# A gate's second half moved beside the next unit's first half, and weight pieces prepared one unit ahead

## The chip, the core and the metric

The kernel runs on one core of a Trainium2 chip. Its metric is device time in microseconds, from a run of the whole program. In what follows, PE is the matrix engine, with its weight loads as a lane of their own (PEld), DVE the vector engine, ACT the scalar engine, POOL the GpSimd engine and SP the engine that issues the DMAs.

## What is computed

Three layers follow one another, all in float32. The kernel reaches float32 accuracy by splitting operands into a high part (rounded to the matrix engine's format) and a low part (what the rounding left), and by three matmuls for each product: high by high, high by low, low by high.

```python
# attention without softmax, 4 batches, 8 heads, 576 positions, head size 64
scores = scale * q @ k.T;  ret = scores * decay_mask;  x = (ret @ v)     # 2304 tokens x 512
# first layer, 512 -> 2048 -> 512
h = x @ w_in;  g = h * cos(h);  x = g @ w_out
# second layer, 512 -> 1536 -> 512
xn = x / rms(x) * rms_g
out = (silu(xn @ w_gate) * (xn @ w_val)) @ w_out
```

## The kernel before, in words

The program has three stages: attention with the first units of the first layer beside it (to about 165 us of the span), the rest of the first layer (to about 510 us), and the second layer (to the end). The change is in the first layer.

**Units.** Tokens are cut into tiles of 512 (the last has 256), the 2048 inner columns into 16 blocks of 128. One unit is one block for one tile. There are 80 units, numbered i, in six segments: 0 to 5, 6 to 21, 22 to 31, 32 to 47, 48 to 63 (the tile of 256 tokens) and 64 to 79. For a unit PE makes 12 matmuls for h (lines 211 to 213, "hidden", called H here, tiles h or acc read from xhi and xlo), and three units later 12 matmuls of the product with w_out (same lines, called O here, read from ghi and glo). In steady state PE's order is H of unit i, O of unit i-3, H of unit i+1, O of unit i-2, and so on. H writes one of four rotating PSUM banks.

**Gate.** Between H and O stands the gate g = h cos h, six instructions that hand over from engine to engine (function gate_cos): ACT rounds h / 2 pi to an integer (line 452, called k here), DVE takes the remainder (line 453, r), ACT the sine (line 455), DVE multiplies by h (line 459), ACT casts to the high part (line 461, tile ghi), and DVE takes the low part (line 135, tile glo; on POOL in units 31 and 47).

**Weight pieces.** Beside units 22 to 67 the weights of the second layer, which come as 64-bit words of two floats' parts, are made into float32: 36 pieces, one for each unit except units 31 and 47, every other unit from 48 to 62, and units 64 to 67. A piece is loaded by SP (line 475, 512 KB), ACT takes the size (line 143) and the low word (line 152), DVE does two bit operations (lines 147 and 148), a combination (line 153) and an addition (line 154), and SP stores it to DRAM (line 491). The function piece_steps is a generator; the gate asks for its next part at five points (step()).

**Other work in the same places.** Units 24 to 62 also carry the root-mean-square normalisation of tiles that are done (tile nt, lines 352 to 396), one or two instructions a unit. Units 68 to 79 carry the splitting of second-layer weights and operands into high and low parts, pulled one by one from a list at the same five points: ACT high part (line 541), DVE low part, four POOL additions on z (line 547), ACT high parts of the sums (line 553), DVE low parts, and ACT and DVE splits of x (line 619 and line 135). At units 46, 47, 62 and 63 the next segment's x is split (ACT line 192, DVE line 135).

**What sets the order.** From unit 22 on, ACT, DVE and POOL run exactly in the order in which the program is written; each engine's queue is in order, so an instruction that waits holds up all behind it. The orders of PE and SP are made by a scheduler when the program is built, and are in order too when it runs.

**Buffers.** The gate's working tile r has two buffers, ghi and glo three each; a piece's raw words have three buffers, its working tile t two. Two pieces are loaded ahead.

Of the kernel before, what the change touches and what calls it, by code (L numbers as in the profile page):

```python
# [30 lines left out]
P = 128  # L31
# [54 lines left out]
def body(ctx: ExitStack, tc, qkv, qkr, vr, w1, w2, rg, gq, gk, mask, out):  # L86
# [35 lines left out]
        taken[0] += 1  # L122
        return hidden_tile() if taken[0] % 2 else acc_tile(KC + taken[0] // 2 % 2)

    mask_sb = const.tile([P, P], F32, name="mask_sb")
# [8 lines left out]
    def minus(eng, dst, hi, src):  # L134
        eng.tensor_tensor(dst, src, hi.bitcast(F32), op=ALU.subtract)  # L135
# [6 lines left out]
    def value1(t, words):  # L142
        nc.scalar.activation(t.bitcast(F32), words[..., 1].bitcast(F32), AF.Abs)

    def value2(t):
        size = t.bitcast(F32)
        nc.vector.tensor_scalar(size, size, LEAST, LARGEST, op0=ALU.max, op1=ALU.min)
        nc.vector.tensor_scalar(t, t, 3, 0x3FFFFFF8, op0=ALU.logical_shift_left, op1=ALU.bitwise_and)

    def value3(t, words):  # L150
        low, high = words[..., 0], words[..., 1]
        nc.scalar.activation(low, low.bitcast(U32), AF.Copy, scale=2.0 ** -29)
        nc.vector.scalar_tensor_tensor(t, high, -2 ** 30, t, op0=ALU.bitwise_and, op1=ALU.bitwise_or)  # L153
        nc.vector.tensor_tensor(t, t, low, op=ALU.add)  # L154
# [73 lines left out]
    N = len(chunks)  # L228
    width = lambda c: P if c < NFULL else REST
    ld, sc, total = {}, {}, {}  # L230
    gam0 = ap1.tile([P, NPAIR, P], F32, name="gam0")
    gam = [gam0]
    PRO = NCH
# [30 lines left out]
    def scores(n):  # L264
        b, c = chunks[n]
        w = width(c)
        kt, qt, vv, _ = ld[n]
        v3 = vv[:w].rearrange("p (h d) -> p h d", h=H)
        nc.gpsimd.tensor_tensor(v3, v3, vg_sb[:w, c, :].unsqueeze(2).to_broadcast([w, H, D]), op=ALU.mult)
        ps = [ps_tile().rearrange("p (h i) -> p h i", h=NPAIR) for _ in range(2)]  # L270
        for p in range(NPAIR):
            for hh in range(2):
                r = slice(hh * D, (hh + 1) * D)
                nc.tensor.matmul(ps[hh][:w, p, :w], kt[r, p, :], qt[r, p, :], start=True, stop=True)  # L274
        for hh in range(2):
# [160 lines left out]
        proj(part1("in", f), t, ps)  # L436
        return ps[:, :n]

    def gate_cos(t, f, ps, between=None, eng=nc.gpsimd, beside=None, copies=()):

        def step():
            next(beside)
            if copies:
                copies.pop(0)()

        n = TILES[t][1]
        r = ch.tile([P, 512], F32, tag="t", name="r")
        k = r.bitcast(I32)
        hi = ch.tile([P, 512], F32R, tag="hi", bufs=LAG, name="ghi")
        lo = ch.tile([P, 512], F32R, tag="lo", bufs=LAG, name="glo")  # L450
        k, r, hi, lo = k[:, :n], r[:, :n], hi[:, :n], lo[:, :n]
# [21 lines left out]
    def piece_load(k):  # L473
        loaded[k] = late["cv"].tile([P, DM, 2], I32, tag="raw", name="raw")
        nc.sync.dma_start(loaded[k].rearrange("p c w -> p (c w)"),
                          w2[k // 2, :, k % 2 * DM:(k % 2 + 1) * DM].bitcast(I32))

    def piece_steps(k):
# [215 lines left out]
    for i in range(LAST + LAG):  # L694
        if i == ATT_STEPS:
            att.close()
            late["psh"] = pool("psh", 1, space=PSUM)
            late["wb"] = mid.enter_context(tc.tile_pool(name="wb", bufs=NSLOT_B, reuse_waits="tile"))
        if ATT_STEPS <= i < MANUAL:
            while len(blocks1) < NW1:  # L700
                blocks1.append(Block(w1[len(blocks1)], wa if len(blocks1) < NSLOT_A else late["wb"]))
        more = [n for n in range(chunk, chunk + CHUNKS[i])] if i < ATT_STEPS else []
        for n in more:
            if n + AHEAD < N:
                fetch_chunks(n + AHEAD)
        early_out = LAG <= i < LAST and i - LAG in ENDS
        if i < LAST:
            s, t, f = STEPS[i]
            ps = hidden(t, f)
            if i in ENDS and i + 1 < LAST:  # L710
                if SEGMENTS[s + 1][1]:
                    fetch_x(SEGMENTS[s + 1][0])
                else:
                    split_x(SEGMENTS[s + 1][0], range(KC // 2, KC) if TILES[t][1] < 512 else range(KC))
            elif i + 1 in ENDS and TILES[t][1] < 512:
                split_x(SEGMENTS[s + 1][0], range(KC // 2))
            if early_out:
                out_t(i - LAG)
            gate_cos(t, f, ps, (lambda: scores(more[0] + 1)) if more and more[0] + 1 < N else None,
                     nc.vector if i < MANUAL or i >= 3 * NF1 or begun(i) is not None else nc.gpsimd,  # L720
                     piece_steps(begun(i)) if begun(i) is not None
                     else other_steps(5 if i < LAST - 1 else 2) if i >= LAST - NF1 else iter(range(5)), late.pop("moves", []))
        elif i >= LAST:
            if i == LAST:

                nc.scalar.activation(spare, half_pi, AF.Silu)
            for _ in range(7):
                pull()
        if i >= LAG and not early_out:
            out_t(i - LAG)  # L730
        if more:
            values(more[0])
            if len(more) > 1:
                if more[0] + 2 < N:
                    scores(more[0] + 2)
                values(more[1])
            chunk += len(more)
        if i < MANUAL:

            while converted[0] < min(len(blocks1), CONVERTED[i]):  # L740
                blocks1[converted[0]].convert(temps())
                converted[0] += 1
        if i == 1:
            keep_x(0)
        if i < LAST - NF1 and (i // NF1 != 3 or 0 not in normal):
            idle()
            idle(1, "D" if i % 2 else "A")
        if i >= LAST - NF1 + LAG:
            ahead(i, i - (LAST - NF1 + LAG))
        if i == MANUAL - 1:  # L750
# [5 lines left out]
            piece_load(0)  # L756
            piece_load(1)
            order = ExitStack()
            order.enter_context(tc.manual_schedule(engines=ENGINES))
# [320 lines left out]
```

## Time and profile before

| | us |
|---|---|
| median of 3 runs | 918.08 (917.05 to 923.83) |
| profiled execution, device time | 917.62 |
| its span, first to last instruction | 915.8 |
| time outside the span | 1.8 |
| PE busy | 890.1 (97%) |
| DVE busy | 666.9 (73%) |
| ACT busy | 476.6 (52%) |
| POOL busy | 91.8 (10%) |

The table's busy times are averages over stages with different limits. A matmul's reported length overlaps the next one's, so the distance between two starts tells more of PE than the length does. A wait is given to the event that came last before the instruction began.

### The profile page before, as it was taken

To read this page: it belongs to the slowest core of one execution; us is meant where nothing else is said; L and a number is where in the kernel's file an instruction comes from. 1 tells how busy PE (TensorE), PEld (TensorE's weight loads), DVE (VectorE), ACT (ScalarE), POOL (GpSimd) and SP (SyncE) were. 2 spreads that over 40 slices of the span, in tenths; PEclk is the share of its full clock that TensorE was granted. 3 is DMA by queue.
4 is the path that set the end of the run, shared out by engine and by line. 5 is a ranking of instruction groups with operands and counts; after the bars stand their busy time and mean duration, and the time that the engine had idled before them with its cause. 6 is when DMAs were issued, how large, how long until landed. Compare 5 with 4: busy or idle time off the path is not lost.

```text
span 915.8 us, 14516 instructions
## 1 busy us (share of the span) xinstructions
PE 890.1 (97%) x5610; PEld 802.0 (88%) x5610; DVE 666.9 (73%) x1003; ACT 476.6 (52%) x819; POOL 91.8 (10%) x99
## 2 busy tenths in 40 slices
PE   7799999999999999989998999999999999999998
PEld 6677787887888887988886999999999999999998
DVE  2999887855878887777777689879675589343484
ACT  3666554745665556646656765536433445333341
POOL 2210010000000000000244444300000000000000
PEclk8999999999999999999999999999999999999999
DMA  8972550504434443332477887998877688866693
GB/s 323 395 298 92 191 212 11 198 11 150 138 108 135 138 138 126 117 104 81 162 236 253 290 315 298 334 340 277 266 259 256 221 278 288 278 246 242 220 295 118
DMA packets 61333, 193.20 MB, mean 211 GB/s; under 512 B 5584, under 2 KB 23632, under 8 KB 52688
## 3 DMA queue, kind: packets, MB, share of 16 engines
q1 hardware_dynamic: 61264, 192.27, 61.3%
q8 instruction: 44, 0.72, 0.3%
q14 instruction: 25, 0.20, 0.1%
HBM read 142.97 MB, written 49.28 MB: 210 GB/s over the span
## 4 chain that ended last, share of the span: by engine, by line
PE 67%; DVE 17%; ACT 7%; issue 4%; DMA 3%; POOL 1%; SPq 1%; ACTq 0%; DVEq 0%; POOLq 0%
PE h L833 13%; PE acc L878 13%; PE acc L833 12%; PE acc L211 5%; PE acc L212 4%; PE acc L213 4%; DVE r L459 2%; PE g L274 2%; PE h L878 2%; DVE w L135 2%; DVE r L453 2%; DVE t L153 2%; ACT ghi L461 2%; PE g L304 2%; DVE t L154 2%
## 5 line engine op out<-in xcount | busy, mean ns | idle before, releaser
L833 PE MATMUL acc<-w 128*128 128x384 f32 x720 | 140.1, 335 | 0.5
L833 PE MATMUL h<-w 128*128 128x384 f32 x720 | 139.8, 335 | 0.8 <-DVE SV L815 0.7
L833 PEld LDWEIGHTS h<-w 128*128 128x128 f32 x720 | 126.1, 188 | 2.4 <-DVE SV L815 1.8
L833 PEld LDWEIGHTS acc<-w 128*128 128x128 f32 x720 | 125.6, 188 | 2.4 <-DVE v L821 2.4
L211 PE MATMUL acc<-ghi,w 128*128 128x512 f32 (+1 forms) x320 | 117.7, 374 | 6.5 <-ACT ghi L461 6.5
L212 PE MATMUL acc<-glo,w 128*128 128x512 f32 (+1 forms) x320 | 119.3, 373 | 0.5 <-DVE glo L135 0.4
L213 PE MATMUL acc<-ghi,w 128*128 128x512 f32 (+1 forms) x320 | 119.0, 372 | 0.0
L878 PE MATMUL acc<-w 128*128 128x256 f32 x846 | 104.2, 283 | 0.0
L878 PEld LDWEIGHTS acc<-w 128*128 128x128 f32 x846 | 103.1, 191 | 0.3 <-DVE w L135 0.2
L455 ACT ACTIVATE r<-r,half_pi 128x512 f32<-128x512 f32 (+1 forms) x80 | 54.5, 682 | 65.1 <-DVE r L453 65.0
L547 POOL TENSOR_TENSOR z<-z 128x256 f32<-128x256 f32 x72 | 63.9, 890 | 164.8 <-DVE r L453 85.4
L135 DVE TENSOR_TENSOR glo<-r,ghi 128x512 fp32r<-128x512 f32 (+1 forms) x78 | 51.5, 661 | 39.1 <-ACT ghi L461 38.6
L211 PEld LDWEIGHTS acc<-ghi,w 128*128 128x128 f32 x320 | 59.9, 188 | 18.5 <-ACT ghi L461 7.9
L461 ACT CAST ghi<-r 128x512 fp32r<-128x512 f32 (+1 forms) x80 | 46.2, 578 | 50.2 <-DVE r L459 47.2
L212 PEld LDWEIGHTS acc<-glo,w 128*128 128x128 f32 x320 | 60.8, 190 | 11.4 <-DVE glo L135 1.5
L213 PEld LDWEIGHTS acc<-ghi,w 128*128 128x128 f32 x320 | 60.9, 190 | 10.2
L821 DVE TENSOR_TENSOR v<-s,acc 128x384 f32<-128x384 f32 x54 | 29.8, 552 | 52.8 <-PE acc L833 39.4
L861 ACT CAST w<-SV 128x768 fp32r<-128x768 f32 x55 | 42.4, 832 | 34.1 <-DVE SV L866 18.2
L135 DVE TENSOR_TENSOR w<-SV,w 128x768 fp32r<-128x768 f32 x55 | 50.3, 957 | 13.5 <-ACT w L861 13.5
L799 ACT COPY s<-h 128x384 f32<-128x384 f32 x54 | 25.9, 480 | 56.6 <-PE h L833 55.2
L799 ACT COPY s<-acc 128x384 f32<-128x384 f32 x54 | 26.0, 481 | 49.6 <-PE acc L833 49.5
L815 DVE TENSOR_TENSOR SV<-s,h 128x384 f32<-128x384 f32 x54 | 29.8, 551 | 27.7 <-PE h L833 22.2
(128 smaller groups left out, 1684.7 us busy)
## 6 DMA issues: line engine op xcount, KB each, us to landing
w<-so SPq DMA_DIRECT2D x42, 768.0 KB, 6.2
w<-s SPq DMA_DIRECT2D x24, 1024.0 KB, 4.9
raw<-w_dram SPq DMA_DIRECT2D x36, 512.0 KB, 4.0
w<-s SPq DMA_DIRECT2D x24, 768.0 KB, 4.3
raw<-w_dram SPq DMA_DIRECT2D x16, 1024.0 KB, 6.6
x<-qkv_dram SPq DMA_DIRECT2D x15, 1024.0 KB, 8.8
s<-w SPq DMA_DIRECT2D x12, 1024.0 KB, 6.3
w<-t SPq DMA_DIRECT2D x36, 256.0 KB, 2.3
```

The source lines that it names most:

```text
L135: eng.tensor_tensor(dst, src, hi.bitcast(F32), op=ALU.subtract)
L211: nc.tensor.matmul(dst, a[0], b[0], start=start, stop=False)
L212: nc.tensor.matmul(dst, a[0], b[1], start=False, stop=False)
L213: nc.tensor.matmul(dst, a[1], b[0], start=False, stop=stop)
L455: nc.scalar.activation(r, r, AF.Sin, bias=half_pi, scale=1.0)
L461: nc.scalar.copy(hi, r)
L547: nc.gpsimd.tensor_tensor(z[:, dst], z[:, a], z[:, b], op=op)
L799: nc.scalar.copy(t[:, :HALF], bank)
L815: nc.vector.tensor_tensor(dst, s, bank, op=ALU.add)
L833: nc.tensor.matmul(bank, w[:, wp, kc * P:(kc + 1) * P], x[:, kc], start=k in (0, 1, 3) and kc == 0 and m == 0, stop=kc == 1 and m == 2, sk ...
L861: nc.scalar.copy(t[:, 0], src)
L878: nc.tensor.matmul(bank, s[:, a, i % 2, m * P:(m + 1) * P], wi[:, b], start=start and i == 0 and p == 0 and m % 2 == 0, stop=i == NPR - 1 ...
```

## The change

In units 22 to 79 the gate's last three instructions (product, cast, low part) no longer follow the sine of the same unit. They are kept as `pending` and are written between the first three of the next unit. The low part is always on DVE. After unit 79 a call without a unit finishes what is pending. For units below 22 the order within a unit stays (`apart` is false).

For a weight piece, the two ACT instructions of piece k+1 are written beside the DVE instructions of piece k; three pieces are loaded ahead and t has three buffers. `mask_sb` moves to a pool that is closed after attention. The number of weight steps that unit 79 and the step behind it pull goes from 2 to 5 and from 7 to 9.

```diff
-    def gate_cos(t, f, ps, between=None, eng=nc.gpsimd, beside=None, copies=()):
+    pending = []
+
+    def gate(t, f, ps, beside, copies, between=None, apart=False):
...
-        nc.scalar.activation(k, ps, AF.Identity, bias=quarter, scale=INV_2PI)
-        nc.vector.scalar_tensor_tensor(r, k, -TWO_PI, ps, op0=ALU.mult, op1=ALU.add)
-        step()
-        nc.scalar.activation(r, r, AF.Sin, bias=half_pi, scale=1.0)
-        step()
-        if between:
-            between()
-        nc.vector.tensor_tensor(r, ps, r, op=ALU.mult)
-        step()
-        nc.scalar.copy(hi, r)
-        step()
-        minus(eng, lo, hi, r)
-        step()
-        g_parts[t, f] = hi, lo
...
+        def finish():
+            mult, cast, low = pending.pop()
+            mult()
+            step()
+            return cast, low
...
+            nc.scalar.activation(k, ps, AF.Identity, bias=quarter, scale=INV_2PI)
+            old = finish() if pending else None
+            nc.vector.scalar_tensor_tensor(r, k, -TWO_PI, ps, op0=ALU.mult, op1=ALU.add)
+            step()
+            if old:
+                old[0]()
+                step()
+            nc.scalar.activation(r, r, AF.Sin, bias=half_pi, scale=1.0)
+            step()
+            if old:
+                old[1]()
+                step()
+            pending.append((lambda: nc.vector.tensor_tensor(r, ps, r, op=ALU.mult), cast, low))
...
+        if pending and (ps is None or not apart):
+            cast, low = finish()
+            cast()
+            step()
+            low()
+            step()
...
     def piece_steps(k):
-        j, n = divmod(k, 2)
-        t = late["cv"].tile([P, DM], I32, tag="t", bufs=2, name="t")
-        value1(t, loaded[k])
+        ahead = piece_first(k + 1) if k + 1 < npiece else []
+        t, words = sizes.pop(k), loaded.pop(k)
         yield
         value2(t)
+        for step in ahead[:1]:
+            step()
         yield
         yield
+        for step in ahead[1:]:
+            step()
+        nc.vector.scalar_tensor_tensor(t, words[..., 1], -2 ** 30, t, op0=ALU.bitwise_and, op1=ALU.bitwise_or)
         yield
-        value3(t, loaded.pop(k))
+        nc.vector.tensor_tensor(t, t, words[..., 0], op=ALU.add)
...
-        if k + 2 < npiece:
-            piece_load(k + 2)
+        if k + 3 < npiece:
+            piece_load(k + 3)
```

Three places of the built programs show what moved. The first is DVE in unit 44, a unit of 512 tokens with a piece beside it (r is the gate's tile, t and raw the piece's). Before:

```order
L453 SCALAR_TENSOR_TENSOR r<-r,acc 128x512
L147 TENSOR_SCALAR t<-t 128x512
L148 TENSOR_SCALAR t<-t 128x512
L459 TENSOR_TENSOR r<-acc,r 128x512
L135 TENSOR_TENSOR glo<-r,ghi 128x512
L153 SCALAR_TENSOR_TENSOR t<-raw,t 128x512
L154 ISA t<-raw,t 128x1024
```

and in the changed program:

```order
L481 TENSOR_TENSOR r<-h,r 128x512
L471 SCALAR_TENSOR_TENSOR r<-r,acc 128x512
L146 TENSOR_SCALAR t<-t 128x512
L147 TENSOR_SCALAR t<-t 128x512
L530 SCALAR_TENSOR_TENSOR t<-raw,t 128x512
L134 TENSOR_TENSOR glo<-r,ghi 128x512
L532 ISA t<-raw,t 128x1024
```

The product (now line 481) and the low part (now line 134) are those of unit 43, whose bank is h; the four piece instructions and the remainder stand between them, and the low part stands between the piece's combination (line 530) and its addition (line 532).

The second is ACT in units 78 (bank h) and 79 (bank acc), the last two. Before:

```order
L452 ACTIVATE r<-h,quarter 128x512
L455 ACTIVATE r<-r,half_pi 128x512
L541 CAST w<-z 128x768
L461 CAST ghi<-r 128x512
L619 CAST w<-xall 128x768
L452 ACTIVATE r<-acc,quarter 128x512
L455 ACTIVATE r<-r,half_pi 128x512
L553 CAST w<-z 128x512 x2
L461 CAST ghi<-r 128x512
L726 ACT_TABLE_LOAD
```

and in the changed program:

```order
L469 ACTIVATE r<-h,quarter 128x512
L462 CAST ghi<-r 128x512
L585 CAST w<-z 128x768
L476 ACTIVATE r<-r,half_pi 128x512
L663 CAST w<-xall 128x768
L469 ACTIVATE r<-acc,quarter 128x512
L597 CAST w<-z 128x512 x2
L462 CAST ghi<-r 128x512
L476 ACTIVATE r<-r,half_pi 128x512
L585 CAST w<-z 128x768
L462 CAST ghi<-r 128x512
L770 ACT_TABLE_LOAD
```

The cast of unit 78 moved behind the rounding of unit 79 and behind the two casts of sums (line 597, before line 553), which stood behind it.

The third is PE at the end of the first layer, from the last O of unit 78 on (h<-w 128x384 is the second layer). Before:

```order
L213 MATMUL acc<-ghi,w 128x512
L833 MATMUL h<-w 128x384 x9
L211 MATMUL acc<-ghi,w 128x512 x4
L212 MATMUL acc<-glo,w 128x512
L213 MATMUL acc<-ghi,w 128x512
```

and in the changed program, from the last matmuls of unit 79's O on:

```order
L210 MATMUL acc<-ghi,w 128x512
L211 MATMUL acc<-glo,w 128x512
L212 MATMUL acc<-ghi,w 128x512
L879 MATMUL h<-w 128x384 x30
L879 MATMUL acc<-w 128x384 x12
```

The nine matmuls of the second layer that stood between the O of units 78 and 79 moved behind unit 79's.

## Rows read from the trace of the kernel before

**Rows 1.** The page's first part: busy time, share of the span, instructions of each engine.
```profile
PE 890.1 (97%) x5610; PEld 802.0 (88%) x5610; DVE 666.9 (73%) x1003; ACT 476.6 (52%) x819; POOL 91.8 (10%) x99
```
**Rows 2.** Busy time by stretch: stretch, its length, five engines' busy us, PE clock, DMA share, GB/s.
```profile
340.00:360.00 20.00, 18.14 (x89) 14.97 (x88) 15.49 (x28) 13.39 (x25) 1.30 (x1) 1.00 0.48 147
...
390.00:420.00 30.00, 26.94 (x179) 24.36 (x178) 23.30 (x48) 14.10 (x30) 0.00 (x0) 0.94 0.32 104
...
480.00:510.00 30.00, 26.00 (x108) 20.80 (x106) 21.17 (x29) 20.77 (x34) 12.70 (x16) 0.94 0.79 264
510.00:600.00 90.00, 88.90 (x506) 86.36 (x505) 74.15 (x109) 54.21 (x106) 35.54 (x42) 1.00 0.86 313
```
**Rows 3.** PE in order of time: start, us, instruction, idle before it.
```profile
352.18 0.39 PE L213 MATMUL acc<-ghi,w 128*128 128x512 f32 x1
353.71 0.38 PE L211 MATMUL acc<-xhi,w 128*128 128x256 f32 x1 [1.14 <-ACT xhi L192]
354.82 0.38 PE L212 MATMUL acc<-xhi,w 128*128 128x256 f32 x1 [0.72 <-DVE xhi L135]
```
**Rows 4.** PE in order of time, round 407 and 413 us.
```profile
406.74 0.28 PE L212 MATMUL acc<-glo,w 128*128 128x256 f32 x1
406.86 0.28 PE L213 MATMUL acc<-ghi,w 128*128 128x256 f32 x1
409.48 0.74 PE L211 MATMUL acc<-ghi,w 128*128 128x256 f32 x4 [2.34 <-ACT ghi L461]
...
412.46 0.63 PE L213 MATMUL h<-xhi,w 128*128 128x512 f32 x1
412.88 0.63 PE L211 MATMUL h<-xhi,w 128*128 128x512 f32 x1
```
**Rows 5.** PE in order of time, at the first layer's end.
```profile
497.91 0.39 PE L213 MATMUL acc<-ghi,w 128*128 128x512 f32 x1
501.90 1.20 PE L211 MATMUL acc<-ghi,w 128*128 128x512 f32 x4 [3.61 <-ACT ghi L461]
```
**Rows 6.** DVE in order of time, from one low part to the next (units 42 and 43).
```profile
330.82 0.69 DVE L135 TENSOR_TENSOR glo<-r,ghi 128x512 fp32r<-128x512 f32 x1 [0.74 <-ACT ghi L461]
...
336.43 0.69 DVE L135 TENSOR_TENSOR glo<-r,ghi 128x512 fp32r<-128x512 f32 x1 [0.74 <-ACT ghi L461]
```
**Rows 7.** Busy time by stretch, as in rows 2, of units 38 to 43 and 55 to 61.
```profile
301.30:336.90 35.60, 35.60 (x159) 29.48 (x158) 30.05 (x52) 18.28 (x32) 0.00 (x0) 1.00 0.43 133
384.00:409.00 25.00, 22.42 (x179) 21.41 (x177) 18.90 (x40) 11.61 (x25) 0.00 (x0) 1.00 0.33 113
```
**Rows 8.** DVE from 384 to 409 us by line: busy us, mean ns, idle before, releaser.
```profile
L135 DVE TENSOR_TENSOR glo<-r,ghi 128x256 fp32r<-128x256 f32 x6 | 2.6, 425 | 3.2 <-ACT ghi L461 3.2
...
L459 DVE TENSOR_TENSOR r<-acc,r 128x256 f32<-128x256 f32 x4 | 1.7, 424 | 2.3 <-ACT r L455 2.3
```
**Rows 9.** ACT from 454 to 502.4 us (units 71 to 78) by line.
```profile
L553 ACT CAST w<-z 128x512 fp32r<-128x512 f32 x10 | 5.9, 619 | 10.7 <-POOL z L547 7.6 <-DMA so<-w 3.1
L455 ACT ACTIVATE r<-r,half_pi 128x512 f32<-128x512 f32 x8 | 5.8, 724 | 4.9 <-DVE r L453 4.9
...
L461 ACT CAST ghi<-r 128x512 fp32r<-128x512 f32 x8 | 5.0, 620 | 3.6 <-DVE r L459 3.5
```
**Rows 10.** ACT in order of time, units 77 and 78.
```profile
493.04 0.82 ACT L541 CAST pw<-z 128x768 fp32r<-128x768 f32 x1
...
496.89 1.14 ACT L553 CAST w<-z 128x512 fp32r<-128x512 f32 x2 [2.33 <-POOL z L547]
497.94 0.68 ACT L452 ACTIVATE r<-h,quarter 128x512 int32<-128x512 f32 x1
...
501.23 0.62 ACT L461 CAST ghi<-r 128x512 fp32r<-128x512 f32 x1 [0.41 <-DVE r L459]
```
**Rows 11.** Line 213 on PE: count, ns min/median/max, first and last start.
```profile
L213 PE MATMUL h<-xhi,w x132: 279/389/628, 167.2 to 486.1; 128*128 128x512 f32 x100, 128*128 128x256 f32 x32
```
**Rows 12.** The page's DMA issues: count, KB each, median us from issue to landing.
```profile
raw<-w_dram SPq DMA_DIRECT2D x36, 512.0 KB, 4.0
```

More of the change, by code (lines that the diff above doesn't have):

```diff
@@ L230, in body @@
     ld, sc, total = {}, {}, {}
+    mask_sb = ap1.tile([P, P], F32, name="mask_sb")
     gam0 = ap1.tile([P, NPAIR, P], F32, name="gam0")
@@ L454, in gate_cos, with cast, low @@
-        step()
-        nc.scalar.activation(r, r, AF.Sin, bias=half_pi, scale=1.0)
-        step()
-        if between:
-            between()
-        nc.vector.tensor_tensor(r, ps, r, op=ALU.mult)
-        step()
-        nc.scalar.copy(hi, r)
-        step()
-        minus(eng, lo, hi, r)
-        step()
-        g_parts[t, f] = hi, lo
+        def finish():
[3 more added lines that the diff above has]
+            return cast, low
+        if ps is not None:
+            n = TILES[t][1]
+            r = ch.tile([P, 512], F32, tag="t", name="r")
+            k, r = r.bitcast(I32)[:, :n], r[:, :n]
+            parts = {}
+            def cast():
+                parts["hi"] = ch.tile([P, 512], F32R, tag="hi", bufs=LAG, name="ghi")[:, :n]
+                nc.scalar.copy(parts["hi"], r)
+            def low():
+                parts["lo"] = ch.tile([P, 512], F32R, tag="lo", bufs=LAG, name="glo")[:, :n]
+                minus(nc.vector, parts["lo"], parts["hi"], r)
+                g_parts[t, f] = parts["hi"], parts["lo"]
+            nc.scalar.activation(k, ps, AF.Identity, bias=quarter, scale=INV_2PI)
[11 more added lines that the diff above has]
+            pending.append((lambda: nc.vector.tensor_tensor(r, ps, r, op=ALU.mult), cast, low))
+            if between:
+                between()
@@ L469, in body @@
+        if pending and (ps is None or not apart):
[4 more added lines that the diff above has]
+            step()
+        for _ in beside:
+            pass
+        while copies:
+            copies.pop(0)()
     store = [dram.tile([P, 4, 2 * P], F32, tag=f"w2_{j}", name=f"w2_{j}") for j in range(NW2)]
@@ L476, in piece_load, with piece_first, size, low @@
                           w2[k // 2, :, k % 2 * DM:(k % 2 + 1) * DM].bitcast(I32))
+    sizes = {}
+    def piece_first(k):
+        def size():
+            sizes[k] = late["cv"].tile([P, DM], I32, tag="t", bufs=3, name="t")
+            value1(sizes[k], loaded[k])
+        def low():
+            words = loaded[k]
+            nc.scalar.activation(words[..., 0], words[..., 0].bitcast(U32), AF.Copy, scale=2.0 ** -29)
+        return [size, low]
     def piece_steps(k):
-        j, n = divmod(k, 2)
-        t = late["cv"].tile([P, DM], I32, tag="t", bufs=2, name="t")
-        value1(t, loaded[k])
+        ahead = piece_first(k + 1) if k + 1 < npiece else []
+        t, words = sizes.pop(k), loaded.pop(k)
         yield
         value2(t)
+        for step in ahead[:1]:
+            step()
         yield
         yield
+        for step in ahead[1:]:
+            step()
+        nc.vector.scalar_tensor_tensor(t, words[..., 1], -2 ** 30, t, op0=ALU.bitwise_and, op1=ALU.bitwise_or)
         yield
-        value3(t, loaded.pop(k))
+        nc.vector.tensor_tensor(t, t, words[..., 0], op=ALU.add)
+        j, n = divmod(k, 2)
         where = store[j][:, 2 * n:2 * n + 2] if j % 3 < 2 else store[j][:, 1:3] if n else store[j][:, 0:4:3]
         nc.sync.dma_start(where, t.bitcast(F32).rearrange("p (n c) -> p n c", n=2))
-        if k + 2 < npiece:
-            piece_load(k + 2)
+        if k + 3 < npiece:
+            piece_load(k + 3)
         yield
@@ L718, in body @@
                 out_t(i - LAG)
[L719 to L722, printed above, removed]
+            gate(t, f, ps, piece_steps(begun(i)) if begun(i) is not None
+                 else other_steps(5) if i >= LAST - NF1 else iter(range(5)), late.pop("moves", []),
+                 (lambda: scores(more[0] + 1)) if more and more[0] + 1 < N else None, i >= MANUAL)
         elif i >= LAST:
             if i == LAST:
+                gate(None, None, None, other_steps(2), [])
                 nc.scalar.activation(spare, half_pi, AF.Silu)
@@ L755, in body @@
             late["cv"] = right("cv", 3)
-            piece_load(0)
-            piece_load(1)
+            for k in range(3):
+                piece_load(k)
             order = ExitStack()
+            for step in piece_first(0):
+                step()
             order.enter_context(tc.manual_schedule(engines=ENGINES))
```

7 lines of the change are left out of this document (removed).

## The prediction

> **What bounds the kernel now.** I read the page's busy shares, then the busy times by stretch, then PE, DVE and ACT in order of time where PE stood still. PE is busy 97% of the span [rows 1], so the whole first layer can only win what PE loses there. It loses it at three places [rows 2]. Where two starts of a matmul lie further apart than usual I count the excess; the usual distance is 0.12 us for 256 columns [rows 4], and for 512 it is 35.6 us over 159 matmuls, 0.22 [rows 7].
>
> First, at 352 us PE waits for the split of x: 353.71 - 352.18 - 0.22 and 354.82 - 353.71 - 0.12, together 2.3 us [rows 3]. Second, from 400 to 414 us it waits for gates of the 256-token segment. The stretch from 390 to 420 has 30 - 26.94 = 3.1 us of idle PE and a granted clock of 0.94 [rows 2]; after the longest wait, 409.48 - 406.86 - 0.12 = 2.5 us, 512-column matmuls start 0.42 us apart instead of 0.22 [rows 4], the 1.2 GHz level. Lost clock is 0.06 of 30 us, 1.8 us, so this place costs 4.9 us. Third, at the end of the layer: from 480 to 510 us there are 4.0 us of idle PE, most of it the 3.6 us before unit 78's O [rows 5], and again a clock of 0.94, 1.8 us [rows 2]: 5.8 us. Together 13.0 us. A reported matmul is longer than the distance to the next, so idle time is counted a little short; I take 13.0 as found and 15 as the most.
>
> Why are the gates late? In units 38 to 43 a unit takes 35.6 / 6 = 5.9 us on DVE and ACT, though DVE works only 30.05 / 6 = 5.0 us and ACT 18.3 / 6 = 3.1 us in it [rows 7], and PE needs 24 x 0.224 = 5.4 us. The rest is a hand-over: in every unit DVE stands 0.74 us for the cast that ACT can only make after DVE's product [rows 6]. A loop of 5.9 behind a PE of 5.4 falls back half a microsecond a unit, until the queue is used up, which is at 352 us. In the 256-token segment PE needs 24 x 0.12 = 2.9 us a unit; DVE and ACT took 25 us for some 6.2 units, 4.0 us each, of which DVE stood 3.2 us for casts and 2.3 us for sines [rows 7, 8]. At the end ACT's rounding of unit 78 starts at 497.94, 11.6 us after that unit's H ended, about 486.3 [rows 10, 11].
>
> **The change, part by part.** No matmul is added or removed, and ACT's and DVE's instructions stay the same but for two low parts that go from POOL to DVE (0.69 us each [rows 6], in units with no piece; hidden by DVE's slack there). All 36 loads remain; the third buffer lets one start earlier.
>
> *Units 22 to 47.* The product comes first in DVE's unit and its cast has the remainder and the piece's instructions (over 2 us of DVE work) to be ready. The 0.74 us go: 336.43 - 330.82 = 5.61 becomes 4.9 [rows 6], under PE's 5.4. The few units that carry two normalisation steps or four additions of x exceed PE's pace for one unit, and fall back in line in the next ones. So no lag builds up, and the split at 352 us is written when its buffers come free, a full O before PE asks for it: 2.3 us won. If DVE had other waits of the same size instead, nothing would be won; I take all, since nothing else holds DVE in these units.
>
> *Units 48 to 63.* DVE's work for a pair of units, one with a piece, is 4.0 x 2 = 8.1 less the waits, 5.5 us over three pairs, or 1.8 each: 6.2 us, against PE's 5.7. So DVE is still the slower one by about 0.25 us a unit where the normalisation runs (units 55 to 61, 1.7 us), and units 61 and 62 have four splits of x more (about 0.6 us each). Against that stands the reserve: between the end of a unit's H and its O, PE does six groups of twelve, 6 x 1.43 = 8.6 us. Pipelining takes one unit of it, 2.9 us, and the low part comes some 3 us into the next unit, so 2.7 us are left, and the lag reaches 2 to 3.5. I keep 1 us of the 4.9 as lost (ends 0 and 3) and win 3.9.
>
> *Units 64 to 79.* Here ACT waits 10.7 us for POOL and for stores at the casts of sums, and 8.5 us for DVE at sines and casts, in 48.4 us and 8 units [rows 9]: 6.0 us a unit. The 8.5 go, since remainder and product are ready a step ahead; the 10.7 stay. (48.4 - 8.5) / 8 = 5.0, under PE's 5.4, so the queue keeps up. But the tail is deeper: unit 78's cast now stands behind its own rounding, the last cast, a high part, 3.85 us from there to the casts of sums (493.04 to 496.89), and these two, 1.05 [rows 10]: about 0.6 + 0.5 + 3.9 + 1.05 + 0.6 = 6.6 us from rounding to high part, where it was 501.85 - 497.94 = 3.9. From unit 78's H to its O PE has four groups of 2.7, 10.9 us. So the tail is free if ACT reaches unit 78 less than 4.3 us late, against 11.6 now. How late it will be follows from unit 77: its high part starts about 1.9 us into the unit (rounding, split of x and cast, 0.5 to 0.7 us each) and the casts of sums end 3.9 + 1.05 us later, 6.8 us for a unit of 5.4; that is 1.4 us late, and up to 3.1 more where a store has to land first, the whole of that wait [rows 9]: 1.4 to 4.5. The nine matmuls that filled the gap moved behind, so a wait there is now wholly lost. I keep 1 us (ends 0 and 5), and win 4.8.
>
> *Pieces ahead.* The size now waits for the load in a step in which cast and sine stand behind it. A load issued at the end of unit i's work, about 5 us into it, is wanted 0.7 us into unit i+2: 2 x 5.4 + 0.7 - 5 = 6.5 us, and it takes 4.0 [rows 12]. Nothing is lost.
>
> *Second layer.* From 510 to 600 us PE loses 1.1 us and the DMA engines are 0.86 busy [rows 2]. Its weights are prepared by the same ACT and DVE queues, which come earlier by more than PE does (the lag of 11.6 us goes as well), so I put this at nothing; the cover is that lead, and if it were gone the DMA share says that some of the gain would be given back there.
>
> **Sum:** 2.3 + 3.9 + 4.8 = 11.0 us, at most 15. The profiled execution was 917.62, so 906.6; the median of the runs is 0.5 higher, 907.1, and of the 2 us between 13 and 15 that the idle times leave out I take one: **906 us**.
>
> **Rivals.** *The tail stays (about 911).* With a reserve one unit smaller and the filler gone, the last units wait as before or more. For it: 7.6 us of ACT's waits are for POOL, which the change doesn't touch [rows 9]. Against: 8.5 us of others go. Then 2.3 + 3.9 are won and the 4.8 not: 911.4. Chance 0.18.
>
> *Nothing changes (914 to 919).* PE is busy 97% and ACT and DVE 52% and 73% [rows 1]; the waits could move to other units, or the second layer could give the gain back at its DMA share of 0.86 [rows 2]. Against it: the idle PE time is there and its releasers are the casts. Beside that stands a rule of the Trainium skill (Perfetto Trace Analysis, Identifying the Most-Contended Engine): find the engine with the highest occupancy and optimise that one first, which is PE here; by it a reordering on DVE and ACT would win nothing, 918. Trace and rule differ as far as DVE, 84% busy in units 38 to 43, sets a pace slower than PE's there. Chance 0.11.
>
> *Slower (927 or more).* ACT's queue blocks on a load: the size of piece k+1 waits for its words, and the last unit's cast, the next sine and so DVE's product stand behind it. Decides from a landing of 6.5 us on. Its place is all 36 pieces; to lose 9 us beyond the 11 won, with some 7 us of reserve to eat first, each must be 0.75 us late, a mean landing of 7.3 us. The median is 4.0 [rows 12], at a DMA share of 0.43 [rows 7]. Chance 0.07. That the change doesn't do what it says is no rival: the built orders show it.
>
> **How the numbers follow.** The forecast has 0.64: 903 (15 won) to 908.8. A measurement of this kernel tells about 1%, 9.2 us, from no change. Faster by over 1% means under 908.9: the forecast and a little of the first rival, 0.66. Within 1%: the other rivals, 0.26. Slower 0.08. The range from 902 to 914 holds the forecast, the first rival and the near end of the second.
>
> **What would show it.** In the changed profile, DVE should show hardly any idle time before the low part, and from 230 to 480 us the rounding should start right behind each H instead of up to 11 us later. PE at about 352 us should go from O to H without a gap. The granted clock should be 1.00 where it was 0.94. If PE still waits several microseconds before the O of unit 78 or 79, the tail was mis-sized; if it waits in units 59 to 63, DVE's work per pair was. If DVE idles before the product instead of the low part, the loop was moved and not cut, and the forecast fails at its first step.

## The result

The changed kernel takes **905.95 us** (median of 6 runs, 903.72 to 907.68) against 918.62 (median of 6 runs, 917.05 to 923.83). The ratio is 0.9852, 95% interval 0.9821 to 0.9882: 12.7 us won, with 10.8 to 16.4 in the interval. The profiled execution took 907.68 us, with a span of 905.9; before it was 917.62 and 915.8.

The page's first line and the busy times by stretch answer to [rows 1] and [rows 2]. The first two stretches hold the places that were at 352 and at 400 to 414 us; the third is the end of the first layer, which now lies at 500 us; the fourth is the start of the second layer.

```profile
PE 888.1 (98%) x5610; PEld 801.2 (88%) x5610; DVE 668.0 (74%) x1005; ACT 472.5 (52%) x819; POOL 89.0 (10%) x97
```
```profile
350.00:370.00 20.00, 20.00 (x112) 17.44 (x111) 14.89 (x32) 12.86 (x28) 0.00 (x0) 1.00 0.30 93
390.00:420.00 30.00, 30.00 (x217) 28.21 (x216) 28.69 (x59) 20.10 (x42) 0.00 (x0) 1.00 0.44 125
470.00:500.00 30.00, 29.61 (x132) 24.28 (x131) 20.98 (x29) 18.12 (x29) 14.16 (x16) 1.00 0.90 301
500.00:590.00 90.00, 89.05 (x508) 86.66 (x507) 73.92 (x108) 54.81 (x107) 32.72 (x38) 1.00 0.80 293
```

PE is busy 20.00 of 20, 30.00 of 30 and 29.61 of 30 us, where it was 18.14, 26.94 and 26.00, and the granted clock is 1.00 at the two places that had 0.94. DVE does 59 instructions in the 30 us of the second stretch where it did 48. The second layer's start loses 0.95 us, as before (1.1). The same three places on PE, in order of time (start, us, instruction, idle before it):

```profile
356.01 0.39 PE L212 MATMUL acc<-ghi,w 128*128 128x512 f32 x1
356.24 0.28 PE L210 MATMUL acc<-xhi,w 128*128 128x256 f32 x1
356.36 0.28 PE L211 MATMUL acc<-xhi,w 128*128 128x256 f32 x1
...
408.05 0.45 PE L210 MATMUL h<-xhi,w 128*128 128x512 f32 x1
408.34 0.28 PE L210 MATMUL acc<-ghi,w 128*128 128x256 f32 x1
...
493.26 0.39 PE L210 MATMUL acc<-ghi,w 128*128 128x512 f32 x1
494.04 0.50 PE L211 MATMUL acc<-glo,w 128*128 128x512 f32 x1 [0.39 <-DVE glo L134]
```

From O to the H that needs the split of x there is no gap any more ([rows 3] had two), unit 61's O at 408.34 starts without the 2.34 us of [rows 4], and of the 3.61 us of [rows 5] 0.39 are left, for a low part instead of a high one.

In DVE's queue, one unit of the stretch of [rows 6]:

```profile
328.77 0.69 DVE L530 SCALAR_TENSOR_TENSOR t<-raw,t 128x512 int32<-128x512 int32 x1
329.38 0.69 DVE L134 TENSOR_TENSOR glo<-r,ghi 128x512 fp32r<-128x512 f32 x1
329.98 0.69 DVE L532 CUSTOM_DVE_ANT_0 t<-raw,t 128x1024 uint16<-128x1024 uint16 x1
330.58 0.75 DVE L396 SCALAR_TENSOR_TENSOR xall<-xall,rg_sb,nt 128x512 f32<-128x512 f32 x1
331.24 0.69 DVE L481 TENSOR_TENSOR r<-acc,r 128x512 f32<-128x512 f32 x1
332.69 0.69 DVE L471 SCALAR_TENSOR_TENSOR r<-r,h 128x512 f32<-128x512 int32 x1 [0.76 <-ACT r L469]
```

The low part has no wait. From unit 22's H to unit 79's H, DVE's waits before the low part sum to 2.2 us, where they were 31.7. The one idle time left in this unit, 0.76 us, is before the remainder, for a rounding that ACT makes as soon as PE has finished H: DVE now waits for PE's pace, as an engine that isn't the bound here.

**How the runs below are compared.** The trace gives finer readings than the median. The *stretch* runs from the start of unit 18's H to the end of unit 79's O: 323.6 us before (322.0 without the nine second-layer matmuls of 0.174 us that stood in it), 307.5 now. *Lag* is the time from the end of a unit's H (its last start and the usual distance) to its rounding on ACT. *Lost* is what starts of matmuls lie further apart than the usual 0.227 us for 512 columns and 0.119 for 256, summed over units; an O counts with the unit whose H stands before it, and matmuls slowed by a lower clock are in it. All are worked out from the traces, one for each kernel. The changed kernel and an exact repeat of it (below) differ by 0.2 us in the stretch and by 0.4 at most in the table's columns of lost. Medians come from different sets of runs, each with runs of the kernel before beside them (medians 918.6 to 920.6); a ratio is always to these. Lost in units 18 to 43 was 0.7 to 1.9 us in every kernel but the one with two buffers (a wait for a fetched x at unit 22), and is left out of the table but for that one.

| kernel | median us | stretch | lag at unit 47, 63, 78 | lost in units 44–49, 50–75, 76–79 |
|---|---|---|---|---|
| before | 918.6 | 323.6 | 4.8, 11.1, 11.5 | 2.4, 6.3, 6.4 |
| changed | 906.0 | 307.5 | 0.2, 3.0, 2.6 | 0.1, 0.9, 0.7 |
| gate alone | 904.8 | 307.9 | 0.2, 3.6, 2.6 | 0.1, 1.0, 0.8 |
| pieces alone | 911.5 | 315.1 | 0.6, 8.2, 9.3 | 0.1, 1.5, 7.3 |
| one instruction moved | 911.0 | 314.3 | 0.9, 9.2, 9.7 | 0.1, 2.5, 5.5 |
| segment in step | 907.6 | 310.3 | 0.2, 8.2, 2.6 | 0.1, 3.2, 0.8 |
| tail in step | 905.1 | 309.1 | 0.2, 3.0, 5.4 | 0.1, 0.6, 1.7 |
| first in step | 906.8 | 311.0 | 5.1, 3.6, 2.7 | 2.8, 1.0, 0.8 |
| low part twice | 905.4 | 308.4 | 0.2, 3.0, 2.8 | 0.1, 0.6, 0.6 |
| low part three times | 911.5 (1 run) | 317.1 | 11.2, 3.6, 2.6 | 8.0, 1.4, 0.7 |
| cast twice | 903.8 | 307.1 | 0.2, 3.0, 2.0 | 0.1, 0.5, 0.0 |
| two buffers of words | 927.1 (1 run) | 330.6 | 9.4, 3.2, 4.4 | 8.7, 1.8, 2.8 (and 12.1 in units 18–43) |

### The profile page after: what moved, and what is told of

It reads as the page before. It is cut to its first block, busy times and chain, and to the rows that moved or that the text cites. A ratio compares the mean times of both kernels' runs of the same rounds, so it can differ in the third digit from the quotient of the medians.

```text
span 905.9 us, 14472 instructions
## 1 busy us (share of the span) xinstructions
PE 888.1 (98%) x5610; PEld 801.2 (88%) x5610; DVE 668.0 (74%) x1005; ACT 472.5 (52%) x819; POOL 89.0 (10%) x97
## 4 chain that ended last, share of the span: by engine, by line
PE 86%; DVE 7%; ACT 3%; issue 2%; DMA 1%; POOL 0%; SPq 0%; ACTq 0%; DVEq 0%; POOLq 0%
PE acc L924 13%; PE h L879 13%; PE acc L879 12%; PE acc L210 9%; PE acc L211 9%; PE acc L212 9%; PE h L211 3%; PE h L210 3%; PE h L212 3%; PE h L924 2%; PE g L274 2%; PE g L304 2%; DVE w L134 2%; PE g L290 2%; PE g L210 1%
## 5 line engine op out<-in xcount | busy, mean ns | idle before, releaser
L210 PEld LDWEIGHTS acc<-ghi,w 128*128 128x128 f32 x320 | 60.3, 189 | 11.2 <-ACT xall L728 0.6
L476 ACT ACTIVATE r<-r,half_pi 128x512 f32<-128x512 f32 (+1 forms) x80 | 54.9, 686 | 14.5 <-DVE r L471 14.2
```

The costliest lines, as they stand in the source:

```text
L210: nc.tensor.matmul(dst, a[0], b[0], start=start, stop=False)
```

## The experiments

**Which half of the change?** The diffs are against the changed kernel unless said otherwise. First the gate without the pieces:

```diff
-        ahead = piece_first(k + 1) if k + 1 < npiece else []
-        t, words = sizes.pop(k), loaded.pop(k)
+        t = late["cv"].tile([P, DM], I32, tag="t", bufs=2, name="t")
+        value1(t, loaded[k])
         yield
         value2(t)
...
+        value3(t, loaded.pop(k))
```

> The gate's product, cast and low part stand beside the next unit as in the changed kernel, but a piece's two ScalarE steps (size, low word) stay in its own unit as in the kernel before. Theory (the stop at the cast is the whole loss): DVE's unit in units 38 to 43 stays at or under 5.3 us, since size and remainder's step give DVE work while ACT makes them; the stretch from unit 18's H to the end of unit 79's O, 323.6 us before and 307.5 after, is 307 to 309 here and the time 905 to 908. Rival (both halves are needed, DVE now stands for the size and the low word instead of the cast, 0.5 us a unit or more): the loop is 5.6 us or more, the gap at the split of x comes back, 911 to 914.

Ratio to before 0.9857 (0.9830 to 0.9883), stretch 307.9: all of the gain. DVE's only wait of size in units 38 to 43 is again that for the rounding; the low part has none, since remainder and bit operations fill the time of the cast:

```profile
323.06 0.69 DVE L471 SCALAR_TENSOR_TENSOR r<-r,acc 128x512 f32<-128x512 int32 x1
323.66 0.42 DVE L146 TENSOR_SCALAR t<-t 128x512 f32<-128x512 f32 x1
324.12 0.43 DVE L147 TENSOR_SCALAR t<-t 128x512 int32<-128x512 int32 x1
324.46 0.69 DVE L134 TENSOR_TENSOR glo<-r,ghi 128x512 fp32r<-128x512 f32 x1
```

Then the pieces without the gate (every unit finishes its own):

```diff
-                 (lambda: scores(more[0] + 1)) if more and more[0] + 1 < N else None, i >= MANUAL)
+                 (lambda: scores(more[0] + 1)) if more and more[0] + 1 < N else None, False)
```

> Every unit finishes its own gate (product, cast, low part) as in the kernel before, but the pieces' ScalarE steps stand one unit ahead, with three loads in flight. Theory: DVE still stands some 0.7 us for the cast in each unit, the loop stays at 5.8 to 5.9 us against PE's 5.44, and the time is that of before, 915 to 920, with the three gaps (split of x, 256-token segment, last O's) of 2, 6 and 6 us back. Rival (the pieces' share of the change is half of the gain): 910 to 914.

The rival was right: 0.9924 (0.9898 to 0.9951), half of the gain, and units 22 to 47 have hardly any lag, although product, cast and low part follow each other within the unit. DVE's queue says why:

```profile
318.63 0.69 DVE L481 TENSOR_TENSOR r<-h,r 128x512 f32<-128x512 f32 x1
319.24 0.68 DVE L530 SCALAR_TENSOR_TENSOR t<-raw,t 128x512 int32<-128x512 int32 x1
320.06 0.69 DVE L134 TENSOR_TENSOR glo<-r,ghi 128x512 fp32r<-128x512 f32 x1
320.67 0.68 DVE L532 CUSTOM_DVE_ANT_0 t<-raw,t 128x1024 uint16<-128x1024 uint16 x1
```

The changed pieces have their L530 between the product and the low part, where before it stood behind the low part. While ACT casts, DVE works, and of the 0.74 us some 0.15 are left. If that is the cause, nothing has to be a unit ahead. So in the kernel *before* this one instruction was moved across the low part:

```diff
         yield
         yield
-        yield
-        value3(t, loaded.pop(k))
+        words = loaded.pop(k)
+        nc.vector.scalar_tensor_tensor(t, words[..., 1], -2 ** 30, t, op0=ALU.bitwise_and, op1=ALU.bitwise_or)
+        yield
+        nc.scalar.activation(words[..., 0], words[..., 0].bitcast(U32), AF.Copy, scale=2.0 ** -29)
+        nc.vector.tensor_tensor(t, t, words[..., 0], op=ALU.add)
```

> The kernel before with one instruction moved: in each piece's unit DVE's combining of the high words with the size (0.69 us, it needs nothing of this unit's cast) stands between the gate's product and its low part instead of behind the low part. No gate is pipelined and no piece step is a unit ahead. Theory (the wait of 0.74 us for the cast cost because no DVE work stood in it; any work of that length that is moved there takes it away): DVE's unit falls from 5.9 to about 5.2 us, the lag in units 22 to 47 stays under 1 us and the gap at the split of x goes, as where the pieces alone were moved ahead: stretch 314.5 to 317, time 910 to 914. Rival (it takes the low word a unit ahead, since DVE waits for it instead): lag of 3 us or more at unit 47, time 915 to 919.

0.9887 (0.9844 to 0.9931), stretch 314.3, lag 0.2 us in units 36 to 46: what the pieces bring alone, from one instruction in each piece.

```profile
315.38 0.69 DVE L459 TENSOR_TENSOR r<-acc,r 128x512 f32<-128x512 f32 x1
315.99 0.68 DVE L488 SCALAR_TENSOR_TENSOR t<-raw,t 128x512 int32<-128x512 int32 x1
316.81 0.69 DVE L135 TENSOR_TENSOR glo<-r,ghi 128x512 fp32r<-128x512 f32 x1
```

This kernel has none of the change's smaller parts (the two low parts that went from POOL to DVE, the weight steps at the end), and its stretch is within 1 us of that of the pieces alone, so these parts show no gain of their own. The two halves remove the same wait. Units without a piece, every second one from 48 on and all from 68 on, have no such instruction to move; there only the pipelined gate helps, and the 256-token segment and the tail are where these two kernels still lose 8 to 9 us.

**Which place?** The gate was put back in step in one region at a time. The three new lines are the segment in step (units 48 to 63), the tail in step (64 to 79) and the first in step (22 to 47, on the kernel with the gate alone); in the first two a unit may also ask for more than its five steps, `next(beside, None)`.

```diff
-                 (lambda: scores(more[0] + 1)) if more and more[0] + 1 < N else None, i >= MANUAL)
+                 (lambda: scores(more[0] + 1)) if more and more[0] + 1 < N else None, i >= MANUAL and i // NF1 != 3)
...
+                 (lambda: scores(more[0] + 1)) if more and more[0] + 1 < N else None, MANUAL <= i < LAST - NF1)
...
+                 (lambda: scores(more[0] + 1)) if more and more[0] + 1 < N else None, i >= 3 * NF1)
```

> As the changed kernel but units 48 to 63 (256 tokens) finish their own gates in step. Theory (the hand-over sets the pace there, the lag before grew from 0.4 us at unit 50 to 11 at unit 63): the gaps before the O of units 59 to 61 and the lower clock behind them come back, 4 to 6 us, and the tail still keeps up: 910 to 912. Rival (the two instructions' places do not matter there, DVE's work of 6.2 us a pair against PE's 5.7 does): lag at unit 63 is 3 to 4 us as in the changed kernel and the time 905 to 907.

> As the changed kernel up to unit 63; units 64 to 79 finish their own gates in step. Theory of the prediction (the tail's 6 us came from the hand-overs in units 64 to 79, where ACT waited 8.5 us for DVE): the lag grows by about 0.5 us a unit to 7 or 8 us at unit 78, over a reserve of some 6 us, so 2 to 6 us are lost before the O of units 77 to 79 and the time is 908 to 912. Rival (the tail was late only because it inherited the 256-token segment's lag): nothing is lost there and the time is that of the changed kernel, 905 to 907.

> The pieces as in the kernel before, and the gate pipelined only from unit 48 on, so that units 22 to 47 are those of before. Theory (each of the three places has a reserve of its own, refilled where a segment ends): the loop of 5.9 us and the gap of 2.4 us at the split of x come back, the lag is under 1 us again at unit 50, nothing more is lost; stretch from unit 18's H to unit 79's O 310 to 311 us against 307.5, time 907 to 909. Rival (lag is handed on from segment to segment, so that the tail pays too): lag at unit 63 over 5 us, 911 or more.

Segment in step: 0.9873 (0.9841 to 0.9905). Its lag does grow to 8.2 us, as the theory said, but from unit 44 on PE loses only 4.0 us against the changed kernel's 1.6, and the pipelined tail works the lag off. The price was between theory and rival. Tail in step: 0.9858 (0.9833 to 0.9883), 2.3 us lost against 1.6: the rival was right that the tail is late mostly because of what it inherits. With both in step (the kernel with the pieces alone, which has no lag before unit 48) the loss is 8.8 us: 7.2 more than in the changed kernel, where the two single ones cost 2.4 and 0.7. (In the other kernels with the changed tail the last column is 0.0 to 0.8, and 2.8 with two buffers, so 0.7 is near what the traces can tell.) The tail's waits in these two kernels, on PE:

```profile
491.53 0.49 PE L210 MATMUL acc<-ghi,w 128*128 128x512 f32 x1 [2.24 <-ACT ghi L462]
492.30 0.50 PE L211 MATMUL acc<-glo,w 128*128 128x512 f32 x1 [0.27 <-DVE glo L134]
495.88 0.50 PE L210 MATMUL acc<-ghi,w 128*128 128x512 f32 x1 [0.77 <-ACT ghi L462]
497.64 0.50 PE L211 MATMUL acc<-glo,w 128*128 128x512 f32 x1 [1.26 <-DVE glo L134]
```
```profile
493.63 0.50 PE L211 MATMUL acc<-glo,w 128*128 128x512 f32 x1 [1.18 <-DVE glo L134]
```

The first four rows are of the kernel with the pieces alone, the last of the tail in step. Segment and tail draw on one reserve: either alone may be late at little cost, not both. First in step: 0.9862 (0.9830 to 0.9894); the gap at the split of x is back, with 2.8 us lost, and the lag is gone by unit 50, so this place stands for itself, as the theory said.

```profile
352.36 0.39 PE L212 MATMUL acc<-ghi,w 128*128 128x512 f32 x1
354.25 0.39 PE L210 MATMUL acc<-xhi,w 128*128 128x256 f32 x1 [1.50 <-ACT xhi L191]
355.36 0.39 PE L211 MATMUL acc<-xhi,w 128*128 128x256 f32 x1 [0.72 <-DVE xhi L134]
```

**Is it DVE's pace, or the hand-over?** Work was added that changes no value:

```diff
-                minus(nc.vector, parts["lo"], parts["hi"], r)
+                for _ in range(2 if MANUAL <= begun_at < 3 * NF1 else 1):
+                    minus(nc.vector, parts["lo"], parts["hi"], r)
```

(`begun_at` is the unit's number.)

> The changed kernel, but in units 22 to 47 the low part is computed twice (the same values), 0.69 us of DVE work more a unit, about what the wait for the cast was. Theory (what counts is DVE's unit, work and waits alike, against PE's 5.44 us): DVE's unit becomes 5.0 + 0.69 = 5.7 us, the lag grows by about 0.25 us a unit from unit 34 on to 3 to 6 us at unit 47, and PE loses 1 to 4 us at the split of x and after: stretch 309 to 313, time 907 to 911. Rival (DVE, 84% busy before, has room for 0.7 us a unit and only the hand-over to ACT and back was harmful): lag stays at 0.2, time 905 to 907.

The same with 3 in place of 2, and the cast (`nc.scalar.copy`) twice in the same way:

> The changed kernel, but in units 22 to 47 the low part is computed three times, 1.38 us of DVE work more a unit. By stretches of four units from unit 24 on the changed kernel has DVE busy 16.5, 18.4, 16.9, 19.9, 19.8, 17.8 us; with 5.5 more each, against PE's 21.8 (22.3 in the third), that is over by 0.2, 2.1, 0.1, 3.7, 3.5, 1.5. Theory (DVE's total work against PE's pace counts, and lag adds up until something needs it): lag of about 10 us at unit 46 or 47, of which some 2.4 are free at the split of x, so PE loses 7 to 9 us in units 44 to 50: stretch 314 to 317, time 911 to 916. Rival (the pace is PE's as long as the reserve of 7 us in the gates holds, and the split is early enough): under 909.

> The changed kernel, but in units 22 to 47 the cast is made twice (the same values), 0.62 us of ScalarE work more a unit. Theory (ACT has 3.1 us of work in a unit of 5.44, and the cast ends 1.1 us before DVE's low part starts): no lag, stretch 307 to 308.5, time 905 to 907. Rival (the hand-overs between the two queues set the pace, whichever engine is lengthened): lag of 2 us or more at unit 47, 908 or more.

Twice: 0.9843 (0.9811 to 0.9875), nothing lost at the split of x. DVE takes the 0.69 us out of its waits for PE. In units 40 to 43:

```profile
308.23:329.99 21.76, 21.76 (x98) 18.02 (x97) 21.31 (x38) 12.26 (x20) 0.00 (x0) 1.00 0.47 146
```

DVE is busy 21.31 of 21.76 us, 98%, and PE doesn't notice; the lag reaches 1.8 us at unit 44 and is 0.3 at 46. My theory had the mechanism and overstated the size: only the stretch with the fullest units goes over PE's pace. Three times, with the work summed by stretches of four units, the sum held: DVE's work goes over PE's pace by 11.1 us, less 2.4 that are free, and 8.0 us were lost in units 44 to 49, with lag 11 to 13 at its highest; 911.5 in its one run. The wait was for a low part of an O rather than for the split of x, and the clock fell behind it:

```profile
352.00:366.00 14.00, 10.99 (x49) 7.96 (x49) 13.54 (x25) 8.05 (x16) 0.00 (x0) 0.88 0.49 157
```
```profile
355.59 0.50 PE L211 MATMUL acc<-glo,w 128*128 128x512 f32 x1 [2.24 <-DVE glo L134]
```

The cast twice: 0.9822 (0.9784 to 0.9860), no lag. Here 0.62 us more on ACT in each unit cost nothing, since DVE has work meanwhile.

**The slower rival: a blocked load.** The first attempt changed what the program asks for, not what runs:

```diff
-        if k + 3 < npiece:
-            piece_load(k + 3)
+        if k + 2 < npiece:
+            piece_load(k + 2)
```

> The changed kernel with two loads in flight as before instead of three, so that the load of piece k+1 is issued only at the end of the unit ahead of the one that makes its size. Theory of the prediction's slower rival (ACT's queue blocks on the load, with cast and sine behind it): the loop is landing 4.1 + size, cast, sine, low word and DVE's last two steps, some 8 us instead of 5.44, so 25 units x 2.7 - 7 of reserve = 60 us, and the pairs of 256-token units, some 9 against 5.7, another 20 to 30: 970 to 1000 us. Rival (a late size only fills time in which ACT idles): under 915.

900.74 us in its one run, stretch 307.7. The expectation rested on an error of mine: "two loads in flight as before" is false. The pool has three buffers of words in both kernels, and the build-time order of SP issues a load as soon as a buffer is free; the instructions of this kernel stand in the same order on every engine as those of the changed one. It is a repeat of the changed kernel, and says only how well the stretch repeats (307.5 and 307.7). What limits loads is the number of buffers:

```diff
-        loaded[k] = late["cv"].tile([P, DM, 2], I32, tag="raw", name="raw")
+        loaded[k] = late["cv"].tile([P, DM, 2], I32, tag="raw", bufs=2, name="raw")
```

> The changed kernel with two buffers for the pieces' words instead of three, so that the load of piece k+2 can only be issued when piece k is done. In the changed kernel's trace piece 23's load is issued at 336.54 us and its size is made at 343.43; with two buffers the load issued there is that of piece 22, whose size was made at 337.99, 1.45 us later, against a landing of 4.1. Theory of the prediction's slower rival: ACT's queue stands for the load with the cast and the sine behind it, the loop is landing 4.1 plus the 4.0 from a size to the end of the piece ahead, some 8 us instead of 5.44: 25 units x 2.6 less 7 of reserve, 58 us, and some 20 more in the 256-token units: 960 to 1000 us. Rival (a late size only fills time in which ACT idles): under 915.

927.1 against 919.5 for before, a run each: slower than before, as that rival said, by its mechanism. ACT in order of time:

```profile
318.48 0.67 ACT L142 ACTIVATE t<-raw 128x512 f32<-128x512 f32 x1 [3.40 <-DMA raw<-w_dram]
319.05 0.61 ACT L462 CAST ghi<-r 128x512 fp32r<-128x512 f32 x1
319.56 0.73 ACT L476 ACTIVATE r<-r,half_pi 128x512 f32<-128x512 f32 x1
...
324.95 0.66 ACT L142 ACTIVATE t<-raw 128x512 f32<-128x512 f32 x1 [3.52 <-DMA raw<-w_dram]
```

The size waits 3.5 us with cast and sine behind it, and the loop is 324.95 - 318.48 = 6.5 us instead of 5.44. I expected 8: the load is issued 2.56 us after a size, not 4.0. DVE has made its combination (line 530) while ACT stood, so low part and addition, which frees the words, follow the size 1.05 us sooner than in the changed kernel, and SP issues the load ahead of the store, 0.4 us sooner:

```profile
318.01 0.69 DVE L530 SCALAR_TENSOR_TENSOR t<-raw,t 128x512 int32<-128x512 int32 x1
319.69 0.69 DVE L134 TENSOR_TENSOR glo<-r,ghi 128x512 fp32r<-128x512 f32 x1 [0.99 <-ACT ghi L462]
320.30 0.69 DVE L532 CUSTOM_DVE_ANT_0 t<-raw,t 128x1024 uint16<-128x1024 uint16 x1
```
```profile
321.05 0.33 SPq L501 DMA_DIRECT2D raw<-w_dram  x1
```

PE loses 25.4 us in all. The third buffer of words is what makes sizes a unit ahead harmless; the change inherited it.

## Why the prediction was right, and where not

**The mechanism and the signs held.** The rounding starts less than 1 us behind each H in units 22 to 60, 0.2 us in most, the gaps at 352 and 409 us are gone, the clock is 1.00, and DVE idles before the remainder, not before the product. In units 61 to 67 the rounding starts 1.0 to 3.1 us behind, so that sign, named up to 480 us, came true for most of the way and not for all.

**The sizes were too small.** Lost by place, before less after, I get 2.4 us at the split of x (forecast 2.3), 5.4 in units 50 to 75 (3.9) and 5.7 in units 76 to 79 (4.8), and 0.9 at unit 22, where all kernels vary: 14.5, near the bound of 15, which allowed for what idle times leave out, and not the 11.0 of the sum. Two terms were short, mainly for one reason: I counted idle time and lost clock, 4.9 us for the second place and 5.8 for the third, where the distances between starts give 6.3 and 6.4. The 1 us that I kept at each was about right: 0.9 and 0.7 were left.

**Why 906 came out none the less.** The start of the program took 4.8 us longer in the profiled run: unit 18's H begins at 191.90 us against 187.13. Nothing there is changed in order, and over the thirteen traces of this study it begins between 185.62 and 191.90, the two ends being the changed kernel and its repeat. So 917.62 - 14.5 + 4.8 leaves 907.9, and 907.68 was measured. On medians, 12.7 us, the error is between the forecast's 11 and the 14.5 of the first layer, and the interval holds both. That the forecast came out to 0.1 us is luck: the sum was some 3.5 us short, and in the profiled run a slow start made up for it; where unit 18 began in the other runs isn't known.

**Units 48 to 63.** A lag of 2 to 3.5 us was forecast for their end, from DVE's 6.2 us a pair; it is 3.0 at unit 63.

**Units 64 to 79: right sum, wrong owner.** "ACT waits 8.5 us for DVE, and these go" is what happens. The lines of ACT over units 71 to 78, which answer to [rows 9]:

```profile
L476 ACT ACTIVATE r<-r,half_pi 128x512 f32<-128x512 f32 x9 | 6.5, 723 | 0.0
L597 ACT CAST w<-z 128x512 fp32r<-128x512 f32 x10 | 5.9, 620 | 9.5 <-POOL z L591 8.2 <-DMA so<-w 1.3
...
L462 ACT CAST ghi<-r 128x512 fp32r<-128x512 f32 x8 | 4.9, 615 | 0.0
```

Sine and cast wait 0.0 us, and the casts of sums keep 9.5 of 10.7. But the step that gave the tail's 4.8 us to these waits fails. With the tail in step ACT waits 7.9 us for DVE again in the same units, and 0.7 us comes back:

```profile
L476 ACT ACTIVATE r<-r,half_pi 128x512 f32<-128x512 f32 x8 | 5.8, 724 | 3.9 <-DVE r L471 3.9
L462 ACT CAST ghi<-r 128x512 fp32r<-128x512 f32 x8 | 5.0, 620 | 4.0 <-DVE r L481 3.9
```

The other part was lag that the 256-token segment handed on, which the sum had booked to that segment alone. Two terms that draw on one reserve can't be priced one by one.

**The tail's depth.** Unit 78 was 2.6 us late, inside the 1.4 to 4.5 forecast, and should have been free up to 4.3. The end lost 0.7 all the same: I took the high part as what O waits for (6.6 us after the rounding; measured 491.71 + 0.62 - 485.05 = 7.3), but O's second matmul needs the low part, and that stands behind two splits of sums on DVE:

```profile
491.32 2.06 DVE L134 TENSOR_TENSOR w<-z,w 128x512 fp32r<-128x512 f32 x2 [0.69 <-ACT w L597]
493.31 0.68 DVE L134 TENSOR_TENSOR glo<-r,ghi 128x512 fp32r<-128x512 f32 x1
```

**Pieces ahead: "nothing is lost" held, its reason was half wrong.** The load's lead is 6.9 us (issued at 336.54, wanted at 343.43), close to the 6.5 worked out. It isn't the least: the last piece's load was issued 4.9 us before its size and landed in 4.8. And "the third buffer lets one start earlier" describes nothing that changed: three buffers of words were there before, with loads issued as far ahead as those allow, and the third buffer that is new holds the sizes. Since the size now stands a unit earlier, the lead fell, from 10.3 us for pieces 16 to 19 to between 6.6 and 6.9. What the pieces bring by themselves, half of the gain, I didn't see at all, because I priced them behind the gate, which had taken the same wait already.

**The rivals.** "Nothing changes" is out. The Trainium skill (Perfetto Trace Analysis, Identifying the Most-Contended Engine) says to optimise the engine of highest occupancy first, and to judge TensorE's headroom by the share of its peak that it reaches and by its weight loads, not by how long its matmuls are busy. By matmuls (97%) or weight loads (88%) [rows 1] that engine is PE, and what the change won is time that PE lost; that nothing on DVE and ACT could win it was my reading and isn't said there. PE got not one instruction fewer, and moving one instruction of 0.68 us in each piece, on an engine that was 73% busy, won 1.1%. Occupancy doesn't lead to that instruction: in units 38 to 43 PE was 100% and DVE 84% busy [rows 7]. What counted there was DVE's unit, waits included, against PE's, since the lag built up in it is paid for later. The slower rival has a real mechanism, which the third buffer of words holds off.

**Second layer.** From the end of unit 79's O to the end it takes 406.7 us before (the nine matmuls added back) and 406.5 after: nothing, as said.

## What to carry to other kernels

Where two in-order engines hand a value to and fro in every unit, look at what stands in each queue between sending and needing it: an independent instruction of about the wait's length, moved there, can fill it (here 0.6 of 0.74 us), and it need not be a stage of a pipeline. Compare each engine's work plus waits per unit with the bound's pace, and then find what needs the result earliest; lag below that reserve was free here, as DVE at 98% shows, and lag above it was lost nearly in full (8.0 of some 8.7 us with the low part three times). Price two edits that remove the same wait, or two places that share a reserve, together: here either half alone gives 1.4% or 0.8%, and both 1.5%.

## What was not expected of the hardware

The start of one and the same order of instructions varies by 6 us between traces, where the second layer takes 405 to 407 us in all of them. The traces come from several chips; those known to be of the same chip differ by some 2 us there, so how much of the 6 is the chip's is open. In the changed kernel's profile and in its repeat, from 30 to 60 us:

```profile
30.00:60.00 30.00, 23.88 (x146) 17.46 (x144) 25.67 (x31) 18.57 (x26) 5.54 (x6) 0.77 0.93 354
```
```profile
30.00:60.00 30.00, 24.51 (x193) 18.17 (x189) 28.32 (x38) 22.58 (x31) 5.46 (x5) 0.89 0.96 364
```

PE is busy for almost the same time, but at a granted clock of 0.77 it gets 146 matmuls done and at 0.89 it gets 193. In both, the DMA engines are over 0.9 busy and PE is idle for some 6 of the 30 us. DVE, too, gets 31 instructions done against 38, so the clock needn't be the cause: it may follow from waits that are longer. What makes it fall further in one run was not tried.
